# Attention with VectorE casts into rows with a gap, a scaled v that goes through PSUM, and another order of the tasks of attention

## The chip, the cores and the metric

One core of a Trainium2 chip runs the whole program. The engines are TensorE (PE; its weight loads are listed as PEld), VectorE (DVE), ScalarE (ACT), GpSimd (POOL) and SyncE (SP, which issues the DMAs). The metric is the device time of one execution in microseconds (us), taken as the median of three runs; lower is better.

## The reference

Three stages follow each other. First attention over 2 x 8 heads, 768 rows, width 64, with a mask: each row of q and k gets a bucket of 6 bits, and only equal buckets attend to each other.

```python
q_bits = (np.einsum('bhsd,dk->bhsk', q, proj) > 0)
k_bits = (np.einsum('bhsd,dk->bhsk', k, proj) > 0)
mask = q_bucket[:, :, :, None] == k_bucket[:, :, None, :]
scores = scale * np.matmul(q, k.transpose(0, 1, 3, 2))
scores = np.where(mask, scores, -1000000000.0)
scores = scores - np.max(scores, axis=-1, keepdims=True)
attn = np.exp(scores)
attn = attn / (np.sum(attn, axis=-1, keepdims=True) + 1e-09)
return np.matmul(attn, v)
```

Then two feed-forward layers on 1536 tokens (512 to 2048 to 512): in the first the middle is a rational function of h (degree 3 over degree 2), in the second it is h minus tanh(h).

## The kernel before

**Attention.** Work goes head by head (16 heads), and in a head in six tiles of 128 keys (j = 0 to 5). What a head needs:

- `split_hi` on ACT and `split_lo` on POOL make two parts, A and Bl, of the loaded k and q; `place` sends them by DMA to TA, TBk and TBq; `bits` (6 matmuls) and its output on DVE write the bucket bits into TBk, and a DMA copies 12 of these rows to TBq.
- `smax`: for each tile two matmuls (`sm`, line 456) and a DVE reduction over 768 columns (`mx`, line 460); when all six are done, `put_max` transposes the maxima (`mt`), DVE writes `mr`, and a DMA puts them into TBq.
- `scores`: for each tile four matmuls (`st`, line 582) into PSUM, then ACT's exponential into an f32 tile `e` (line 585).
- `round_e` rounds `e` to f16 (`eh`). `EH_ACT` says how many of the 768 columns ACT takes in each of the six tiles, 768, 768, 128, 768, 512, 768; DVE casts the rest (line 593), so 640 columns in tile 2 and 256 in tile 4. `rest_e` forms `el = e - eh` on POOL (line 602). The last head has tables of its own (`EH_ACT_LAST`, `EL_DVE_LAST`), by which DVE does some of the `el`.
- `attend`: 18 matmuls for each tile (`pv`, lines 634 to 637), with pieces of `eh` and `el` as weights.
- v is scaled by a power of two and split in two: `vhi` on ACT (line 548), `vlo` on DVE in one instruction that reads v and the high part, both in SBUF (line 557; heads 0 and 1 take ACT and POOL). `vmean_of` makes the mean over v.

**PSUM.** `double` gives one of three buffers of two banks, used in turn by `sm`, `st`, `bits`, `xT`, the shifted weight words (`low`) and, at the end, `hr`. So a matmul into the next buffer waits until the engine that reads the third last one is done. `single` gives one bank for small things; one more bank holds `pv`.

**What sets the order.** Every task gets a place on a common scale (one unit is one tile j, six are a head): the tables `T` and `EARLY` give its offset, lines 686 to 748 make the list, and lines 749 and 750 sort it and record the instructions in this order. Each engine runs its own instructions strictly in that order; semaphores are set from the data. `fill` (line 607) issues matmuls on constants into an unused part of the `pv` bank; `FILL` says where and how many.

**Seam.** While the last heads run, the weights of the first layer are prepared (ACT `scale`, DVE `low` and `wt`, lines 187 and 192, ACT and POOL halves). After the last scores four `hr` tiles (unit 0 of the first layer) and the rest of `pv` run, then the last `xT` transposes, then `h` of unit 1 begins. From there on a planner of the same kind (`NUDGE` shifts single tasks) orders the two layers.

Of the kernel before, what the change touches and what calls it, by code (L numbers as in the profile page):

```python
# [11 lines left out]
AF = mybir.ActivationFunctionType  # L12
# [21 lines left out]
M = dict(a=1, b=3.35, c=3.69, d=5, e=5, y=1.59, scale=3.71, join=3.82, halves=6.35)  # L34
# [16 lines left out]
EARLY = {0: dict(load=-61.69, hi=-62.14, lo=-60.39, place=-60.58, bits=-58.96, bits_out=-57.68, place_a=-58.4,
                lead=52.54, put=-46.37, v=-63.23, vmax=-58.62, vall=-56.52, vscale=-54.29, vhi=-6.88,
                vlo=-6.75, vmean=-5.12, vmean_out=-2.89, vback=-56.49, vagain=-55.68, put_half=-47.77,
                ls=0.86),
         1: dict(load=-67.13, hi=-65.44, lo=-65.19, place=-64.04, bits=-59.08, bits_out=-58.81, place_a=-57.52,
                lead=54.94, ls=1.12),
         2: dict(load=-64.89, hi=-61.91, lo=-61.61, place=-61.57, place_a=-61.53, bits=-58.68, bits_out=-58.14,
                lead=9.66, v=-20.61, ls=1.03),
         3: dict(load=-22.52, hi=-15.52, lo=-14.68, place=-14.44, place_a=-13.73, bits=-12.32, bits_out=-11.43,
                lead=9.64)}  # L60
NE = 1
T_LAST = dict(norm=9.87, x=10.11, x_out=10.68)

# [21 lines left out]
 'x_hi 0 5 0': -0.33,  # L85
 't_sum 1 5 0 3': -0.73}
GC = dict(sub=0.7, hi=1.35, lo=1.95)
# [35 lines left out]
def tile_fn(ctx: ExitStack, tc: tile.TileContext, kq, v, proj, w1i, w1o, a_, b_, w2i, w2o, out):  # L123
# [197 lines left out]
    with ExitStack() as actx:  # L321
# [228 lines left out]
        def vlo(h):  # L550
            t = VB[h % 3]
            if h in VLO_POOL:
# [65 lines left out]
        def attend(h, j):  # L618
# [561 lines left out]
```

## Time and profile before

| what | us |
|---|---|
| median of 3 runs (lowest, highest) | 766.49 (766.38, 767.56) |
| the profiled execution: time, span of its instructions | 770.33, 768.5 |
| PE busy, share of the span | 740.6, 96% |
| DVE busy | 625.3, 81% |
| POOL busy | 556.4, 72% |
| ACT busy | 492.6, 64% |

The profile is of one execution, a little slower than the median; its span leaves out 1.83 us around the instructions. Busy shares are means over stages with different limits; a matmul's end is modelled, so a busy PE can still contain short waits. The clock shown (PEclk) is the share of full speed that TensorE was granted.

### The profile page before, as it was taken

How to read it: one execution, taken by the hardware profiler on the slowest of the kernel's cores; microseconds unless marked ns; L12 is line 12 of the kernel's file. 1: busy time of each engine (PE TensorE's matmuls, PEld its weight loads, DVE VectorE, ACT ScalarE, POOL GpSimd, SP SyncE). 2: the span in 40 equal slices, each digit the busy share in tenths (PEclk: the TensorE clock that was granted, in tenths of full speed). 3: DMA queues.
4: the chain of work that ended last, by engine and by line, in shares of the span. 5: the costliest groups of instructions: out<-in, count | busy, mean ns of one | idle time of the engine just before them, and what ended most of it. 6: DMA issues, size and time to landing. Idle time of an engine off the chain costs nothing.

```text
span 768.5 us, 13965 instructions
## 1 busy us (share of the span) xinstructions
PE 740.6 (96%) x5273; PEld 639.6 (83%) x5273; DVE 625.3 (81%) x988; ACT 492.6 (64%) x831; POOL 556.4 (72%) x458
## 2 busy tenths in 40 slices
PE   5999999999998899999999999999999999999997
PEld 3888888888786788888888888887989899989886
DVE  6688999999988888879899998999656766767655
ACT  2577888878896788776666677767554354344421
POOL 3498999898998687787777789968555465465621
PEclk9699999999999999999999999999999999999999
DMA  7573546537421231121121212201031220311003
GB/s 195 147 181 108 146 130 166 158 93 191 119 85 55 71 95 56 55 82 56 57 81 56 82 29 64 73 1 56 27 110 41 70 82 28 110 55 55 28 28 137
DMA packets 41051, 66.52 MB, mean 87 GB/s; under 512 B 3844, under 2 KB 27492, under 8 KB 40984
## 3 DMA queue, kind: packets, MB, share of 16 engines
q1 hardware_dynamic: 40984, 65.63, 29.4%
q8 instruction: 41, 0.67, 0.4%
q14 instruction: 26, 0.21, 0.1%
HBM read 43.00 MB, written 3.15 MB: 60 GB/s over the span
## 4 chain that ended last, share of the span: by engine, by line
PE 77%; DVE 12%; POOL 4%; issue 2%; ACT 2%; DMA 1%; SPq 0%; ACTq 0%; DVEq 0%; POOLq 0%
PE y L1005 17%; PE y L784 12%; PE h L262 12%; PE st L582 7%; PE h2b L922 6%; PE h2e L922 4%; PE h2a L922 4%; PE sm L456 3%; DVE mx L460 3%; PE bits L431 2%; PE hr L262 2%; PE pv L634 1%; PE pv L635 1%; DVE eh L593 1%; PE pv L637 1%
## 5 line engine op out<-in xcount | busy, mean ns | idle before, releaser
L602 POOL TENSOR_TENSOR el<-e,eh 128x768 f16<-128x768 f32 (+1 forms) x95 | 158.8, 1687 | 26.1 <-ACT eh L591 15.1
L1005 PE MATMUL y<-wO,G 128*128 128x512 f32 x576 | 145.1, 393 | 0.3 <-POOL G L990 0.3
L990 POOL TENSOR_TENSOR G<-tmp,G 128x384 fp32r<-128x384 f32 x64 | 66.1, 1034 | 95.6 <-ACT G L985 85.6
L1005 PEld LDWEIGHTS y<-wO,G 128*128 128x128 f32 x576 | 107.0, 188 | 19.1 <-POOL G L990 0.8
L585 ACT ACTIVATE e<-st,lnk 128x768 f32<-128x768 f32 x96 | 86.2, 899 | 29.8 <-PE st L582 26.6
L460 DVE TENSOR_REDUCE mx<-sm 128x1 f32<-128x768 f32 x96 | 90.2, 951 | 9.6 <-PE sm L456 8.4
L1020 DVE TENSOR_TENSOR ya<-y,ya 128x512 f32<-128x512 f32 x84 | 58.1, 692 | 34.5 <-PE y L1005 34.5
L318 POOL TENSOR_TENSOR G<-vec,G 128x512 fp32r<-128x512 f32 x44 | 57.1, 1304 | 26.1 <-ACT G L313 26.0
L591 ACT CAST eh<-e 128x768 f16<-128x768 f32 (+2 forms) x93 | 65.8, 708 | 1.9
L784 PE MATMUL y<-G,wO 128*128 128x512 f32 x288 | 66.7, 389 | 0.0
L784 PE MATMUL y<-G,wE 128*128 128x512 f32 x288 | 66.3, 389 | 0.0
L262 PE MATMUL h<-x,wO 128*128 128x512 f32 x288 | 66.3, 389 | 0.0
L582 PE MATMUL st<-TA 128*128 128x384 f32 x192 | 57.5, 381 | 6.3 <-DVE wt L192 3.3
L784 PEld LDWEIGHTS y<-G,wE 128*128 128x128 f32 x288 | 54.1, 188 | 11.2
L262 PEld LDWEIGHTS h<-x,wO 128*128 128x128 f32 x288 | 54.1, 188 | 11.2
L784 PEld LDWEIGHTS y<-G,wO 128*128 128x128 f32 x288 | 54.0, 188 | 11.1
L634 PEld LDWEIGHTS <-eh 128*128 128x128 f16 x576 | 53.4, 97 | 9.2 <-issue 8.7
L634 PE MATMUL pv<-VB,eh 128*128 128x65 f16 x540 | 59.5, 195 | 0.0
L635 PE MATMUL pv<-VB,eh 128*128 128x64 f16 x540 | 59.1, 196 | 0.0
L637 PE MATMUL pv<-VB,el 128*128 128x65 f16 x540 | 58.6, 193 | 0.4 <-POOL el L602 0.4
L922 PE MATMUL h2b<-x,wE 128*128 128x384 f32 x288 | 58.1, 336 | 0.6 <-DVE tmp L938 0.6
L456 PE MATMUL sm<-TBk,TBq 76*128 76x384 f32 x192 | 54.7, 372 | 3.4 <-DVE mx L460 2.0
(170 smaller groups left out, 1877.4 us busy)
## 6 DMA issues: line engine op xcount, KB each, us to landing
raw<-in_w1i_dram SPq DMA_DIRECT2D x16, 512.0 KB
raw<-in_w1o_dram SPq DMA_DIRECT2D x16, 512.0 KB
raw<-in_w2i_dram SPq DMA_DIRECT2D x16, 512.0 KB
raw<-in_w2o_dram SPq DMA_DIRECT2D x16, 512.0 KB
kq<-in_kq_dram SPq DMA_DIRECT2D x16, 384.0 KB
TA<-A SPq DMA_DIRECT2D x32, 192.0 KB
TA<-Bl SPq DMA_DIRECT2D x32, 192.0 KB
vraw<-in_v_dram SPq DMA_DIRECT2D x8, 384.0 KB
```

What stands on the lines that cost most here:

```text
L262: nc.tensor.matmul(ps, l[:, dc], r, start=(n == 0), stop=(n == 11))
L456: nc.tensor.matmul(ps[:, n], TBq[h][0:76, j * P:(j + 1) * P], TBk[h][0:76, n * SH:(n + 1) * SH], start=True, stop=True)
L460: d = nc.vector.tensor_reduce(mx[h][:, j:j + 1], ps, axis=AX.XY, op=ALU.max)
L582: nc.tensor.matmul(ps[:, n], l[h][0:k, j * P:(j + 1) * P], q[h][0:k, n * SH:(n + 1) * SH], start=(k == P), stop=(k < P))
L585: outs["e", (h, j)] = lambda: nc.scalar.activation(halved(e), ps, AF.Exp, scale=1.0 / math.sqrt(D), bias=lnk)
L602: nc.gpsimd.tensor_sub(el[h, j][:, n:S], e[:, n:S], eh[h, j][:, n:S])
L634: nc.tensor.matmul(out(t), a[:, q], vb[:, j, 0:PW], start=False, stop=False, skip_group_check=True)
L635: nc.tensor.matmul(out(t)[:, 0:D], a[:, q], vb[:, j, PW:PW + D], start=False, stop=False, skip_group_check=True)
L637: nc.tensor.matmul(out(t), l[:, q], vb[:, j, 0:PW], start=False, stop=(j == NK - 1), skip_group_check=True)
L784: nc.tensor.matmul(ps, l[:, o], r, start=(n == 0), stop=(n == 11))
L922: nc.tensor.matmul(banks[n, k], w_in(j, l)[:, o:o + P], x[:, r, dt], start=new and z == 0, stop=z == 5, skip_group_check=not new)
L1005: nc.tensor.matmul(ps, g[:, l, o], r, start=(z == 0), stop=(z == 5))
```

## The change

It does six things.

1. `EH_ACT` gives ACT 384 columns of tile 4 (before 512), so DVE casts 384 (before 256); tile 2 stays at 640 on DVE. In tiles that DVE shares, `eh` is laid out in rows of 128 with a pitch of 130 (`EP`), so that DVE's casts write 5 and 3 rows of 128 with a gap of two elements, from one unbroken run of `e`.
2. `vlo` (heads 2 to 15): ACT writes the scaled v into columns 0 to 383 of the single bank, now one fixed tile `sbank`, and DVE subtracts the high part from it. `single` hands out columns 384 to 511 of the same bank.
3. In `vall` the maximum over a pair of heads is written to SBUF instead of PSUM.
4. The last head's tables: DVE gets `el` of 640, 640 and 512 columns and fewer casts.
5. `FILL`: nine places instead of three, 205 matmuls instead of 96.
6. New numbers in `T`, `EARLY`, `T_LAST` and ten more `NUDGE`s; a function `before` only asserts that the sorted tasks stand in a legal order.

```diff
-EH_ACT = (768, 768, 128, 768, 512, 768)
+EH_ACT = (768, 768, 128, 768, 384, 768)
+EP = P + 2
-EH_ACT_LAST = (0, 0, 768, 0, 640, 768)
-EL_DVE_LAST = (128, 0, 0, 128, 128, 768)
-FILL = ((1.54, 30), (100.1, 16), (200, 50))
+EH_ACT_LAST = (128, 0, 768, 768, 768, 768)
+EL_DVE_LAST = (640, 0, 0, 640, 512, 0)
+FILL = ((1.54, 28), (199.95, 68), (102.13, 12), (-62.29, 25), (-56.14, 20), (-45.0, 12), (92.46, 26), (-26.05, 8),
+ (55.32, 6))
...
+        sbank = sgl.tile([P, 512], F32, name="sbank")
+        user = []
         def single(name):
-            return sgl.tile([P, 512], F32, name=name, tag="s")
+            user[:] = [name]
+            return sbank[:, SH:512]
+        def still(name):
+            assert user == [name], (user, name)
...
             def back():
-                m = ps[0:2, P + 8:P + 9]
-                nc.vector.tensor_reduce(m, ps[0:2, 0:P], axis=AX.X, op=ALU.max)
-                nc.vector.tensor_mul(dg, ident[0:2, 0:2], m.to_broadcast([2, 2]))
+                still(f"vt{pr}")
+                nc.vector.tensor_reduce(dg[:, 2:3], ps[0:2], axis=AX.X, op=ALU.max)
+                nc.vector.tensor_mul(dg[:, 0:2], ident[0:2, 0:2], dg[:, 2:3].to_broadcast([2, 2]))
...
         def vlo(h):
...
-            nc.vector.scalar_tensor_tensor(out=t[:, :, D + 1:2 * D + 1], in0=vsl(h), scalar=vsc[h],
-                                           in1=t[:, :, 0:D], op0=ALU.mult, op1=ALU.subtract)
+            x = sbank[:, 0:SH].rearrange("p (t d) -> p t d", t=NK)
+            nc.scalar.activation(x, vsl(h), AF.Copy, scale=vsc[h])
+            nc.vector.tensor_sub(t[:, :, D + 1:2 * D + 1], x, t[:, :, 0:D])
...
         def round_e(h, j):
-            eh[h, j] = ap.tile([P, S], F16, name=f"eh{h}_{j}", tag="eh", bufs=6)
+            t = ap.tile([P, NK * EP], F16, name=f"eh{h}_{j}", tag="eh", bufs=6)
             n = (EH_ACT if h < BH - 1 else EH_ACT_LAST)[j]
+            w = P if n == S else EP
+            t = eh[h, j] = t[:, 0:NK * w].rearrange("p (t w) -> p t w", w=w)[:, :, 0:P]
+            r, e = n // P, ef[h, j].rearrange("p (t w) -> p t w", w=P)
             if n:
-                nc.scalar.copy(eh[h, j][:, 0:n], ef[h, j][:, 0:n])
+                nc.scalar.copy(t[:, 0:r], e[:, 0:r])
             if n < S:
-                nc.vector.tensor_copy(eh[h, j][:, n:S], ef[h, j][:, n:S])
+                nc.vector.tensor_copy(t[:, r:NK], e[:, r:NK])
```

Three places show how the order moves. The first is DVE in the opening, from the bits of head 1 to the bits of head 2 (`mx_211` and `mx_257` are the maxima of head 0, `mx_248` and `mx_316` those of head 1). Before:

```order
L441 TENSOR_SCALAR TBk_183<-bits_200,thr,amp 44x768
L460 TENSOR_REDUCE mx_211<-sm_4_245 128x1
L460 TENSOR_REDUCE mx_248<-sm_0_249 128x1
L460 TENSOR_REDUCE mx_211<-sm_5_254 128x1
L476 TENSOR_SCALAR mr_0_263<-mt_0_261 3x128
L460 TENSOR_REDUCE mx_248<-sm_1_258 128x1
L460 TENSOR_REDUCE mx_248<-sm_2_267 128x1
L476 TENSOR_SCALAR mr_3_280<-mt_3_278 3x128
L441 TENSOR_SCALAR TBk_237<-bits_270,thr,amp 44x768
```

And now:

```order
L537 TENSOR_SCALAR TBk_210<-bits_239,thr,amp 44x768
L556 TENSOR_REDUCE mx_257<-sm_4_291 128x1
L573 TENSOR_SCALAR mr_0_299<-sbank 3x128
L556 TENSOR_REDUCE mx_257<-sm_5_295 128x1
L573 TENSOR_SCALAR mr_3_311<-sbank 3x128
L537 TENSOR_SCALAR TBk_282<-bits_303,thr,amp 44x768
L556 TENSOR_REDUCE mx_316<-sm_0_317 128x1
```

The three maxima of head 1 that stood ahead of the last `mr` of head 0 now stand behind it.

The second is DVE in a middle head (tile 4 of head 4; `VB` is the low part of v). Before:

```order
L460 TENSOR_REDUCE mx_1125<-sm_2_1244 128x1
L593 CAST eh_4_1271<-e_4_1238 128x256
L570 SCALAR_TENSOR_TENSOR VM_147<-vm_1247,VM_147 32x64
L460 TENSOR_REDUCE mx_1125<-sm_3_1280 128x1
L441 TENSOR_SCALAR TBk_1234<-bits_1264,thr,amp 44x768
...
L557 SCALAR_TENSOR_TENSOR VB_138<-vraw_558,vsc_867,VB_138 128x6x64
```

And now:

```order
L556 TENSOR_REDUCE mx_1203<-sm_2_1310 128x1
L671 SCALAR_TENSOR_TENSOR VM_148<-sbank,VM_148 32x64
L537 TENSOR_SCALAR TBk_1314<-bits_1319,thr,amp 44x768
L697 CAST eh_4_1331<-e_4_1302 128x3x128
L658 TENSOR_TENSOR VB_139<-sbank,VB_139 128x6x64
L556 TENSOR_REDUCE mx_1203<-sm_3_1371 128x1
```

The bits of the next head stand ahead of the cast, and the low part of v directly behind it.

The third is ACT at the same place. Before:

```order
L585 ACTIVATE e_4_1238<-st_4_1239,lnk 128x768
L591 CAST eh_4_1271<-e_4_1238 128x512
L569 ACTIVATE VM_147<-vm_1247 64x64
L585 ACTIVATE e_5_1274<-st_5_1275,lnk 128x768
```

And now:

```order
L686 ACTIVATE e_4_1302<-st_4_1303,lnk 128x768
L670 ACTIVATE VM_148<-sbank 64x64
L695 CAST eh_4_1331<-e_4_1302 128x3x128
L657 ACTIVATE sbank<-vraw_619,vsc_946 128x384
L686 ACTIVATE e_5_1334<-st_5_1335,lnk 128x768
```

The copy of the scaled v is one instruction more between the exponentials of tiles 4 and 5.

On SP the copy of the bits to TBq now stands ahead of the four copies to TA of the same head, and no longer behind them. On PE the fills stand: 25 ahead of the first `bits`, 20 behind the first `vt` transpose, 12 and 8 among the maxima of head 1, 28 behind tile 1 of head 0, 6 in head 9, 26 behind tile 2 of the last head, and 80 in one row behind the last `xT` (before: 30 in head 0, 16 ahead of the last `xT` and 50 behind it).

## Rows read from the trace of the kernel before

**Rows 1.** Busy time by stretch: PE, PEld, DVE, ACT, POOL, then PEclk, DMA, GB/s.

```profile
225.35:260.16 34.81, 29.66 (x360) 25.14 (x356) 29.09 (x42) 25.74 (x42) 27.88 (x21) 0.95 0.14 47
260.16:768.50 508.34, 501.90 (x2352) 432.05 (x2352) 399.44 (x629) 295.74 (x539) 344.35 (x312) 1.00 0.20 64
```

**Rows 2.** The same view from head to head (first scores to first scores).

```profile
26.57:215.25 188.68, 182.39 (x2357) 161.50 (x2355) 169.16 (x265) 156.86 (x231) 167.47 (x99) 0.98 0.53 142
...
54.02:68.18 14.16, 14.16 (x172) 12.80 (x172) 11.88 (x20) 9.95 (x15) 10.86 (x8) 0.88 0.29 68
...
81.96:94.42 12.46, 12.46 (x174) 11.39 (x172) 11.80 (x22) 10.97 (x18) 11.20 (x8) 1.00 0.47 115
94.42:107.86 13.44, 13.32 (x177) 11.66 (x175) 12.16 (x18) 11.47 (x18) 12.79 (x8) 1.00 0.62 167
...
146.16:160.61 14.45, 13.70 (x178) 11.73 (x176) 13.73 (x18) 12.26 (x20) 12.95 (x8) 1.00 0.48 131
```

**Rows 3.** Timeline around 52 us: start, length, engine, line, tiles, wait before.

```profile
50.80 1.65 POOL L602 TENSOR_TENSOR el<-e,eh 128x768 f16<-128x768 f32 x1
50.99 1.60 DVE L593 CAST eh<-e 128x256 f16<-128x256 f32 x1
...
52.88 1.08 DVE L441 TENSOR_SCALAR TBk<-bits,thr,amp 44x768 fp32r<-44x768 f32 x1
...
54.02 0.62 PE L582 MATMUL st<-TA 128*128 128x384 f32 x2 [1.37 <-DVE TBk L441]
```

**Rows 4.** Busy time by stretch of 2 us, behind that stall.

```profile
56.00:58.00 2.00, 2.00 (x10) 1.74 (x10) 0.91 (x2) 1.53 (x2) 1.04 (x2) 0.50 0.67 193
```

**Rows 5.** Groups of DVE by form: count, busy us, mean ns, idle before.

```profile
L187 DVE TENSOR_SCALAR low<-raw 128x512 int32<-128x512 int32 x64 | 43.9, 686 | 0.1
...
L593 DVE CAST eh<-e 128x256 f16<-128x256 f32 x15 | 19.4, 1295 | 0.2 <-ACT e L585 0.2
...
L593 DVE CAST eh<-e 128x640 f16<-128x640 f32 x15 | 12.9, 862 | 1.0 <-ACT e L585 1.0
L557 DVE SCALAR_TENSOR_TENSOR VB<-vraw,vsc,VB 128x384 f16<-128x384 f32 x14 | 12.8, 916 | 0.2
...
L651 DVE TENSOR_TENSOR xt<-pv,rz 128x384 f32<-128x384 f32 x15 | 8.4, 557 | 0.5
```

**Rows 6.** DVE line 593 by itself: lengths in ns, least/median/most.

```profile
L593 DVE CAST eh<-e x34: 483/1017/1943, 34.9 to 238.8; 128x640 f16<-128x640 f32 x15, 128x256 f16<-128x256 f32 x15, 128x768 f16<-128x768 f32 x3, 128x128 f16<-128x128 f32 x1
```

**Rows 7.** DVE line 600 by itself, the same columns.

```profile
L600 DVE TENSOR_TENSOR el<-e,eh x4: 278/1094/1553, 230.6 to 240.4; 128x128 f16<-128x128 f32 x3, 128x768 f16<-128x768 f32 x1
```

**Rows 8.** ACT line 554 by itself, the same columns.

```profile
L554 ACT ACTIVATE vx<-vraw,vsc x2: 600/606/612, 17.1 to 31.6; 128x384 f32<-128x384 f32 x2
```

**Rows 9.** Timeline of PE in the opening.

```profile
26.57 0.99 PE L582 MATMUL st<-TA 128*128 128x384 f32 x2
...
29.28 3.08 PE L615 MATMUL pvw<-ones 128*128 128x122 f16 x30
...
32.22 0.60 PE L582 MATMUL st<-TA 128*128 128x384 f32 x2
```

**Rows 10.** Timeline of DVE in the opening.

```profile
14.76 6.14 DVE L460 TENSOR_REDUCE mx<-sm 128x1 f32<-128x768 f32 x7
...
23.57 0.28 DVE L476 TENSOR_SCALAR mr<-mt 3x128 fp32r<-3x128 f32 x1 [0.74 <-PE mt L471]
```

**Rows 11.** Timeline around the seam.

```profile
232.12 1.75 DVE L593 CAST eh<-e 128x768 f16<-128x768 f32 x1
...
235.35 0.59 PE L582 MATMUL st<-TA 128*128 128x384 f32 x2 [2.58 <-DVE wt L192]
```

**Rows 12.** Timeline of PE at the end of the seam.

```profile
255.81 2.83 PE L615 MATMUL pvw<-ones 128*128 128x122 f16 x50
260.16 2.12 PE L262 MATMUL h<-x,wE 128*128 128x512 f32 x8 [1.52 <-DVE g L308]
```

**Rows 13.** Timeline of PE at the entry of the second layer.

```profile
503.36 2.35 PE L922 MATMUL h2a<-x,wE 128*128 128x384 f32 x12 [1.43 <-ACT tmp L933]
```

More of the change, by code (lines that the diff above doesn't have):

```diff
@@ L51 @@
[L51 to L60, printed above, removed]
+T = {'load': -21.6,
+ 'hi': -16.1,
+ 'lo': -15.12,
+ 'place': -13.78,
+ 'place_a': -12.96,
+ 'bits': -13.59,
+ 'bits_out': -13.11,
+ 'put': -3.09,
+ 'put_out': -3.08,
+ 'vhi': -8.16,
+ 'vlo': -6.69,
+ 'vmean': -2.55,
+ 'vmean_out': -1.12,
+ 'lead': 9.84,
+ 'max': 0.3,
+ 'exp': 0.41,
+ 'round': 0.91,
+ 'rest': 1.08,
+ 'pv': (5.03, 6.95, 7.8, 8.64, 8.0, 9.16),
+ 'pv_last': (5.41, 6.77, 8.07, 9.01, 8.9, 9.11),
+ 'norm': 9.95,
+ 'x': 14.6,
+ 'x_out': 15.0,
+ 'v': -16.72,
+ 'vmax': -12.1,
+ 'vall': -10.56,
+ 'vscale': -9.62,
+ 'h0': 0.65,
+ 'slot': 0.93,
+ 'a': 0.78,
+ 'b': 2.0,
+ 'c': 2.29,
+ 'd': 4.03,
+ 'e': 4.29,
+ 'gates': 21.86,
+ 'vback': -10.2,
+ 'vagain': -9.93,
+ 'w_load': 7.03,
+ 'wt': (-41.69, -21.14, -17.84, -12.15, -6.33, -4.04, 0.32, 3.85),
+ 'ls': 0.98}
@@ new lines @@
+EARLY = {0: {'load': -61.72,
+     'hi': -61.83,
+     'lo': -60.39,
+     'place': -60.47,
+     'bits': -58.96,
+     'bits_out': -54.6,
+     'place_a': -58.76,
+     'lead': 52.4,
+     'put': -46.8,
+     'v': -63.23,
+     'vmax': -58.62,
+     'vall': -56.59,
+     'vscale': -54.29,
+     'vhi': -6.88,
+     'vlo': -6.21,
+     'vmean': -4.7,
+     'vmean_out': -2.89,
+     'vback': -56.5,
+     'vagain': -55.68,
+     'put_half': -47.77,
+     'ls': 0.87,
+     'x': 14.61},
+ 1: {'load': -66.87,
+     'hi': -65.63,
+     'lo': -65.13,
+     'place': -64.04,
+     'bits': -61.45,
+     'bits_out': -58.61,
+     'place_a': -57.52,
+     'lead': 51.27,
+     'ls': 1.45,
+     'vagain': -10.0,
+     'vlo': -3.71},
+ 2: {'load': -64.89,
+     'hi': -61.83,
+     'lo': -61.61,
+     'place': -61.6,
+     'place_a': -61.53,
+     'bits': -59.14,
+     'bits_out': -58.33,
+     'lead': 9.69,
+     'v': -20.69,
+     'ls': 1.13,
+     'vall': -10.56},
+ 3: {'load': -22.46,
+     'hi': -15.52,
+     'lo': -15.12,
+     'place': -14.51,
+     'place_a': -13.12,
+     'bits': -12.26,
+     'bits_out': -11.13,
+     'lead': 9.99,
+     'ls': 1.0}}
@@ L61 @@
 NE = 1
-T_LAST = dict(norm=9.87, x=10.11, x_out=10.68)
+T_LAST = {'norm': 9.87, 'x': 10.11, 'x_out': 11.11}
 NUDGE = {'stage_e 10 1': 1.68,
@@ L85 @@
  'x_hi 0 5 0': -0.33,
- 't_sum 1 5 0 3': -0.73}
+ 't_sum 1 5 0 3': -0.73,
+ 'x_hi 1 1 0': -0.21,
+ 'stage_c 11 1': 0.92,
+ 'stage_b 10 3': -0.56,
+ 'u2 0 0': -0.74,
+ 'join1 4 0': 0.76,
+ 'x_lo 0 5 0': -0.15,
+ 'y2_out 1 1': -0.02,
+ 'rest2 3 1': 2.41,
+ 'x_lo 0 0 0': 5.11,
+ 'scale2 3 1': -1.22}
 GC = dict(sub=0.7, hi=1.35, lo=1.95)
@@ L469, in put_part @@
         def put_part(h, m, t0, n):
-            ps = single(f"mt{h}_{t0}")[0:n, 0:P]
+            ps = single(f"mt{h}_{t0}")[0:n]
             nc.tensor.transpose(ps, m[:, t0:t0 + n], ident)
             def out():
+                still(f"mt{h}_{t0}")
                 mr = ap.tile([n, P], F32R, name=f"mr{h}_{t0}", tag="mr", bufs=2)
@@ L567, in out @@
             def out():
+                still(f"vm{h}")
                 t, c = VM[h % 3], 2.0 ** 14 * EPS / S
@@ L633, in attend @@
                 q = slice(t * P, (t + 1) * P)
-                nc.tensor.matmul(out(t), a[:, q], vb[:, j, 0:PW], start=False, stop=False, skip_group_check=True)
-                nc.tensor.matmul(out(t)[:, 0:D], a[:, q], vb[:, j, PW:PW + D], start=False, stop=False,
+                nc.tensor.matmul(out(t), a[:, t], vb[:, j, 0:PW], start=False, stop=False, skip_group_check=True)
+                nc.tensor.matmul(out(t)[:, 0:D], a[:, t], vb[:, j, PW:PW + D], start=False, stop=False,
                                  skip_group_check=True)
```

59 lines of the change are left out of this document (42 added, 17 removed).

## The prediction

> **What bounds the kernel now.** I read the busy times by stretch first, then those from head to head, then the timeline where a head is long, then the DVE groups by form. From 260.16 us on PE is busy for 501.90 of 508.34 us [rows 1]: the two layers are bound by matmuls, and the change hardly touches them. What can move is attention and seam, 0 to 260 us.
>
> In a middle head without disturbance PE is busy all the time, 12.46 of 12.46 us, and 13.32 of 13.44 us in the next, which also carries the transposes of a pair [rows 2]. So 12.95 us is what PE itself wants for a head, as the mean of the two. Fourteen heads took 188.68 us [rows 2] instead of 14 x 12.95 = 181.3: 7.4 us are lost to waits and to a low clock, in some heads only. The head at 146.16 us took 14.45 us, and DVE was busy for 13.73 of them [rows 2]. There DVE is the late engine, since the weights of the first layer pass through it as well.
>
> How DVE makes PE late stands in one place as an example [rows 3]. POOL works on `el` from 50.80 to 52.45; DVE's cast of 256 columns starts at 50.99 and ends 0.14 us after POOL, at 52.59. Behind it in the queue stands TBk, which empties a PSUM buffer; the next scores wait for it and start at 54.02, after 1.37 us without a matmul. [...]
>
> That the cast is held and not slow is seen from the groups: 256 columns took 1295 ns on average, 640 columns only 862 [rows 5], and the shortest cast 483 ns [rows 6]. The old `vlo` (two inputs in SBUF) took 916 ns, while an instruction of the same 384 columns with one input in PSUM took 557 [rows 5].
>
> **The change part by part.** *Casts.* Tile 4: 384 columns in 3 rows. No cast of this form stands in the trace. Bounds: below, that it runs as the shortest one, under 0.48 us; above, that it is still held as before, 1.3 us for the mean and 1.94 for the worst [rows 5, 6]. I take the pace of DVE operations at one column a cycle: 512 columns in 686 ns and 384 in 557 [rows 5], so 0.55 us for 384 and, by the same slope of 1.0 ns a column, 0.82 for 640. Tile 2 then gains 0.04 us in the mean and tile 4 0.75, and neither depends on POOL any more.
>
> [...]
>
> *vlo.* 916 ns become 557 by the row of the same size with one input in PSUM [rows 5]: 0.36 us of DVE. ACT pays: one copy of 384 columns, 0.61 us [rows 8], less about 0.1 for the 128 columns it gives up. Here the destination is PSUM and not SBUF, which I cannot price apart; I take the same. ACT was busy for 156.86 us in 14 heads, 11.2 of 13.5 us a head [rows 2], so 0.5 more is hidden at 11.7 of 12.95. It adds a wait too: DVE's subtraction waits for ACT's copy, and behind it on DVE stands the maximum of tile 3, for which the next `sm` waits. I count it at nothing, because DVE gets back 0.04 + 0.75 + 0.36 = 1.15 us a head. That cover is gone where the weights are prepared; then up to 0.6 us a head shows.
>
> *Order in the middle heads.* TBk now stands ahead of the cast of tile 4 (second fence of the change), so the stall of rows 3 should not occur even if the cast is slow. SP sends the bits ahead of the four copies to TA; those are needed by scores a head later, so their later issue is hidden. Of the 7.4 us of loss I take 60%, 4.5 us (range 1 to 6.5): the rest is short waits that another queue order makes anew.
>
> *Opening.* The last `mr` of head 0 stood behind nine maxima and now stands behind six. Seven took 6.14 us, 0.88 each [rows 10], so it ends 2.6 us earlier than 23.85. But the scores also stand behind all `sm` of head 1, which DVE paces, so I take 1.2 us off the first scores' start at 26.57 [rows 9]. From there 32.22 - 26.57 = 5.65 us go into eight score matmuls and 30 fills, which ran at 0.103 us each, against 2.83 / 50 = 0.057 later [rows 9, 12]. With the new fills ahead of them (25 + 20 + 12 + 8, all where PE waits for DMA or DVE) part of this may run at the full clock: up to 2.8 us, of which I take 0.8, since DVE's pace still leaves gaps. Together 2.0 (range 0 to 4.5).
>
> *Seam.* At 232 us a cast of 768 columns took 1.75 us, and the scores waited 2.58 us for the weight word behind it [rows 11]. Now DVE has ahead of that word a cast in 5 rows (0.82), an `el` of 640 (0.82) and a cast of 768 in 6 rows, an even count, which I leave at 1.75 as before. The `el` has two inputs in SBUF: line 600, 128 columns wide, took between 278 and 1553 ns [rows 7], so it too can be held, by 1.27 us. I take 2.0 us off the wait, less 0.5 that the 26 new fills (26 x 0.057 = 1.5) and the held `el` cost: 1.5 (range -1 to 3).
>
> [...]
>
> At the end of the seam nothing is won: 50 fills end at 258.64 and `h` waits until 260.16 [rows 12]; the 80 fills now behind `xT` last 80 x 0.057 = 4.6 us against 1.5 + 2.83, and `h` now waits for a weight word behind the same `g`.
>
> *Second layer.* `h2a` waits 1.43 us for ACT behind a chain of DVE [rows 13], and one subtraction of DVE (`x_lo 0 0 0`) is moved out of it, 5 us later, by its `NUDGE`: 0.5 us (range -0.5 to 1.4). *Fills* in the middle: 6 x 0.057 = 0.3 us more on a busy PE.
>
> **Sum.** 4.5 + 2.0 + 1.5 + 0.5 - 0.3 = 8.2 us. The profiled execution took 770.33 us, so it would take 762.1; the median of the runs is 3.84 lower, 766.49, and gives 758.3.
>
> **Rivals.**
> (a) *The relief is taken up by the next wait.* ACT and POOL are close behind: POOL was busy for 167.47 us in 14 heads, 12.0 us of the 12.95 that PE wants [rows 2]. If they set the pace in half of the heads, two thirds of the 4.5 are lost: 8.2 - 3.0 = 5.2 less at best; with the opening unchanged (2.0), 3.2: 763.3 us. Against it: el itself does not grow, and POOL too waits less when casts end early.
> [...]
> (c) *Slower: ACT's copy falls on the path.* It stands between the exponentials of tiles 4 and 5, and each exponential frees a PSUM buffer for coming matmuls. If PE waits for it in each of 14 heads, it costs 14 x 0.6 = 8.4 us, and each stall can bring a stretch at the lower clock as in rows 4; with three of these, 1.0 us each (2 us at half the clock), it is 11.4 against 8.2: 766.49 + 3.2 = 769.7. It decides once ACT needs more than the 12.95 us of PE, that is 1.2 us more than my 11.7, in most heads; so far it needs that at most in the stretch from 146 us on, where it was busy for 12.26 of 14.45 [rows 2].
> (d) *More than forecast*: the opening at full clock (4.5), all of the middle (6.5), the seam 3: 15 with the rest, 751.5.
>
> **How the numbers follow.** Forecast 0.60, (a) 0.13, (b) 0.08, (c) 0.10, (d) 0.06, nothing that can be told 0.03. About 0.2%, 1.5 us, is what a measurement of this kernel tells from no change. Faster by more: forecast, (a), (b), (d), less 0.02 from their edges: 0.85. Within: 0.05. Slower: 0.10. The likeliest case by itself reaches from 754 to 762. The range goes to 752 for (d), and to 766 to take in (a) and (b) with the upper bounds of their terms; (c) is left out.
>
> **What would show it.** Right: in the profile after, casts of 384 near 0.55 us and of 640 near 0.82 with hardly any spread; `VB` on DVE near 0.56; the head at 146 us near 13.4; no stretch at half clock near 56 us; first scores near 25 us. Wrong: casts that still spread from 0.5 to 1.9 us (b); ACT above 12.5 us a head and PE waiting for `e` (c); first scores at 26.5 with the clock at half until 32. I would be wrong as a whole if the heads, although DVE waits less, still take 13.4 us and more.

## Result and the profile after

The changed kernel takes 757.52 us (median of 4 runs, 756.77 to 761.38) against 766.62 us for the kernel before in the same session: a ratio of 0.9889, 95% interval 0.9859 to 0.9918. Its profiled execution is the slowest of the four, 761.38 us with a span of 759.6. A second session gave 757.00 us (754.63 to 757.55) and a ratio of 0.9852 (0.9834 to 0.9871). That profile (754.63 us, span 752.9) is of the fastest of its four executions, so the two bracket the others. Stages are compared below within profiled executions, from the first scores of one head to those of another. So that they can be added, this is the first one against that of before:

| stretch | before, us | after, us | difference | predicted |
|---|---|---|---|---|
| start to first scores | 26.57 | 25.88 | -0.7 | -1.2 |
| heads 0 and 1 | 27.45 | 30.46 | +3.0 | -0.8 (clock) |
| heads 2 to 14 | 171.33 | 163.51 | -7.8 | -4.5, fills +0.3 |
| head 15 to first `h` (seam) | 34.81 | 31.43 | -3.4 | -1.5 |
| `h` to the end | 508.34 | 508.32 | 0.0 | -0.5 |
| sum | 768.5 | 759.6 | -8.9 | -8.2 |

Busy time by stretch of the kernel after; columns as in [rows 1]. The stretches are heads 0 and 1, head 2, head 3, the head that answers to 146.16 of [rows 2], fourteen heads, the seam, and all that follows:

```profile
25.88:56.34 30.46, 28.40 (x282) 25.82 (x278) 18.71 (x32) 22.42 (x34) 20.67 (x13) 0.78 0.40 117
56.34:69.15 12.81, 12.57 (x179) 11.46 (x175) 11.92 (x22) 10.98 (x17) 11.44 (x7) 1.00 0.49 129
69.15:81.62 12.47, 12.47 (x176) 11.74 (x176) 10.43 (x18) 11.71 (x19) 11.43 (x7) 1.00 0.62 164
145.05:158.00 12.95, 12.95 (x183) 11.90 (x182) 11.54 (x20) 12.39 (x20) 12.32 (x8) 1.00 0.60 157
25.88:209.18 183.30, 179.13 (x2363) 163.89 (x2360) 155.68 (x265) 160.49 (x244) 159.83 (x99) 0.96 0.54 146
219.85:251.28 31.43, 29.80 (x400) 25.89 (x397) 24.34 (x41) 26.82 (x45) 25.58 (x21) 1.00 0.16 52
251.28:759.60 508.32, 501.83 (x2355) 432.21 (x2352) 396.62 (x629) 295.69 (x539) 344.29 (x312) 1.00 0.20 64
```

A head with the transposes of a pair takes 12.47 us now (69.15 us), where [rows 2] had 13.44 (94.42 us). Head 2, without them, took 14.16 behind the stall of [rows 3] and takes 12.81. Over fourteen heads DVE is busy 155.68 us instead of 169.16, ACT 160.49 instead of 156.86. The stretch that lost is the first: heads 0 and 1 at a mean clock of 0.78.

DVE by form in the kernel after (count, busy us, mean ns, idle before), against [rows 5]:

```profile
L697 DVE CAST eh<-e 128x640 f16<-128x640 f32 x16 | 13.0, 812 | 2.8 <-ACT e L686 2.8
L697 DVE CAST eh<-e 128x384 f16<-128x384 f32 x15 | 8.3, 554 | 0.5
L658 DVE TENSOR_TENSOR VB<-sbank,VB 128x384 f16<-128x384 f32 x14 | 7.8, 560 | 0.5
L610 DVE TENSOR_TENSOR vdg<-ident,vdg 2x2 f32<-2x2 f32 x8 | 6.2, 781 | 0.3
L704 DVE TENSOR_TENSOR el<-e,eh 128x640 f16<-128x640 f32 x2 | 1.8, 886 | 0.1
```

The casts and `VB` have the durations that the prediction gave (0.82, 0.55, 0.56). The fourth row is a cost that it did not count: `vdg` is the product of `ident` and the maximum of v (`back` in the diff), which now takes that maximum from SBUF, and this product of 2x2 elements takes 0.78 us in the mean, up to 1.65, where it took 0.145 before.

The opening of this execution, in PE's timeline and by stretch:

```profile
27.02 0.51 PE L683 MATMUL st<-TBq,TBk 77*128 77x384 f32 x2
29.59 0.27 PE L605 MATMUL sbank<-ident,vm 128*2 128x128 f32 x1 [2.06 <-DVE vm L596]
29.70 2.30 PE L719 MATMUL pvw<-ones 128*128 128x122 f16 x28
```

```profile
26.00:30.00 4.00, 1.94 (x17) 1.64 (x16) 2.42 (x5) 3.79 (x6) 1.29 (x1) 1.00 0.82 282
32.00:44.00 12.00, 12.00 (x67) 10.70 (x68) 6.44 (x12) 7.62 (x12) 8.13 (x7) 0.50 0.40 99
54.00:58.00 4.00, 4.00 (x57) 3.67 (x57) 3.87 (x7) 3.48 (x7) 3.56 (x3) 1.00 0.42 105
```

PE waits 2.06 us for the maximum of the second pair's v, and from 32 to 44 us it works without a break at a granted clock of 0.50, where the kernel before had 1.00 from 32 us on. The stall of [rows 3] and the half clock of [rows 4] at 54 to 58 us are gone.

### The profile page after: what moved, and what is told of

The parts are those of the page before. It is cut to its first block, busy times and chain, and to the rows that moved or that the text cites. A ratio compares the mean times of both kernels' runs of the same rounds, so it can differ in the third digit from the quotient of the medians.

```text
span 759.6 us, 14193 instructions
## 1 busy us (share of the span) xinstructions
PE 740.5 (97%) x5382; PEld 645.3 (85%) x5382; DVE 604.4 (80%) x985; ACT 497.9 (66%) x847; POOL 546.2 (72%) x459
## 4 chain that ended last, share of the span: by engine, by line
PE 71%; DVE 15%; POOL 4%; ACT 4%; DMA 2%; issue 2%; SPq 0%; ACTq 0%; POOLq 0%; DVEq 0%
PE y L1140 17%; PE y L919 14%; PE h L351 13%; PE h2b L1057 7%; DVE mx L556 5%; PE h2e L1057 4%; PE h2a L1057 4%; PE st L683 3%; PE sm L552 2%; ACT e L686 2%; PE bits L527 1%; DVE TBk L537 1%; POOL G L407 1%; POOL wE L976 1%; DVE eh L697 1%
## 5 line engine op out<-in xcount | busy, mean ns | idle before, releaser
L706 POOL TENSOR_TENSOR el<-e,eh 128x768 f16<-128x768 f32 (+2 forms) x96 | 152.8, 1610 | 29.3 <-ACT eh L695 13.0
L556 DVE TENSOR_REDUCE mx<-sm 128x1 f32<-128x768 f32 x96 | 89.4, 949 | 15.5 <-PE sm L552 14.8
L919 PEld LDWEIGHTS y<-G,wO 128*128 128x128 f32 x288 | 54.0, 188 | 11.1
L738 PE MATMUL pv<-VB,eh 128*128 128x65 f16 x540 | 57.8, 193 | 0.0
L739 PE MATMUL pv<-VB,eh 128*128 128x64 f16 x540 | 57.4, 195 | 0.0
```

The lines of the kernel that those rows point to most:

```text
L556: d = nc.vector.tensor_reduce(mx[h][:, j:j + 1], ps, axis=AX.XY, op=ALU.max)
L706: nc.gpsimd.tensor_sub(l[:, r:NK], e[:, r:NK], eh[h, j][:, r:NK])
L738: nc.tensor.matmul(out(t), a[:, t], vb[:, j, 0:PW], start=False, stop=False, skip_group_check=True)
L919: nc.tensor.matmul(ps, l[:, o], r, start=(n == 0), stop=(n == 11))
```

## Experiments

All ratios are to the kernel before in the same session. "Middle" is heads 2 to 14, from the first scores of head 2 to those of head 15 in the profiled execution.

| kernel | casts | vlo | order | median, us | ratio (95%) | middle, us |
|---|---|---|---|---|---|---|
| before | one run | old | old | 766.5 to 768.2 | 1 | 171.3 |
| after, again | gap | PSUM | new | 757.00 | 0.9852 (0.9834 to 0.9871) | 163.5 |
| nogap | one run | PSUM | new | 764.32 | 0.9956 (0.9940 to 0.9971) | 171.1 |
| evenrows | gap, 6 and 2 rows | PSUM | new | 766.67 | 0.9983 (0.9972 to 0.9993) | 172.2 |
| gap_t2 | gap in tile 2 only | PSUM | new | 757.96 | 0.9865 (0.9842 to 0.9887) | 162.5 |
| vlo_old | gap | old | new | 759.88 | 0.9893 (0.9867 to 0.9918) | 164.7 |
| order_alone | one run | old | new | 770.70 | 1.0037 (1.0022 to 1.0052) | 171.3 |
| before_gap | gap | old | old | 768.26 | 0.9996 (0.9977 to 1.0014) | 166.4 |
| gap_bank | gap, not in head 12 | old | old | 764.85 | 0.9959 (0.9944 to 0.9974) | 167.0 |
| old_order | gap | PSUM | old | 773.85 | 1.0068 (1.0043 to 1.0094) | 172.5 |
| old_order_vlo | gap | PSUM, earlier | old | 772.88 | 1.0058 (1.0037 to 1.0080) | 175.0 |
| fill_first | gap | PSUM | new | 757.76 | 0.9857 (0.9835 to 0.9880) | 164.1 |
| fill_vdg | gap | PSUM | new | 755.08 | 0.9824 (0.9802 to 0.9845) | 161.7 |

### after_again: the changed kernel a second time

> The changed kernel once more, to see whether the opening of its first profile is the rule. In that profile PE stood for 2.06 us ahead of 29.59 us, until v of the second pair had come and DVE had its maximum, and then TensorE had 0.50 of its clock from about 31 to 44 us, with PE busy all the time; that execution took 761.4 us, the others 756.8 to 758.0. Theory: the low stretch is there in every execution and only its length differs, so a profile of some 757 us shows it shorter (clock 0.50 for 6 to 10 us instead of 13). Rival: it is an accident of that one execution; then the clock stays at 1.00 from 24 us on. Time by both: 757.5 us, 756.5 to 761.

By stretch:

```profile
14.00:21.00 7.00, 6.22 (x25) 4.11 (x24) 5.28 (x8) 1.85 (x3) 2.67 (x2) 0.57 0.94 226
30.00:44.00 14.00, 13.37 (x161) 11.64 (x161) 10.18 (x16) 13.04 (x20) 13.10 (x9) 1.00 0.51 141
25.33:49.64 24.31, 22.68 (x281) 20.31 (x278) 19.56 (x32) 22.47 (x34) 20.56 (x13) 1.00 0.49 138
49.64:213.13 163.49, 160.56 (x2244) 146.63 (x2240) 143.84 (x246) 148.13 (x226) 148.93 (x93) 1.00 0.54 145
```

The rival was right on the stretch: 1.00 from 30 to 44 us. Heads 0 and 1 took 24.31 us instead of 30.46, and all of the 6.7 us between the two spans lies before head 2; the middle agrees within 0.02 us. So the opening is decided by the execution (head 2 starts at 49.6 to 56.3 us), the middle is not. PE's wait for the maximum of v was shorter here, 0.99 us instead of 2.06, and the clock did not fall behind it:

```profile
27.98 0.27 PE L605 MATMUL sbank<-ident,vm 128*2 128x128 f32 x1 [0.99 <-DVE vm L596]
```

### nogap and evenrows: what the gap and the odd count do

```
-EP = P + 2
+EP = P
```

> The changed kernel with the gap taken out (rows of eh 128 wide again, so source and destination of every cast are one run). Theory: the casts are held by POOL again; 384 columns spread from about 0.4 to 1.9 us with a mean above 0.9, 640 columns from 0.48 to 1.9; DVE is busier by some 10 us in 16 heads, POOL's el spreads up to 2.0 us as before, and the time rises by 2 to 5 us, to about 761. Rival: the new order made the gain and hides the held casts: the spread returns and the time stays within 1.5 us of 757.5.

```
-EH_ACT = (768, 768, 128, 768, 384, 768)
+EH_ACT = (768, 768, 0, 768, 512, 768)
```

> The gap stays, but DVE casts 768 columns of tile 2 (6 rows) and 256 of tile 4 (2 rows) in place of 640 (5 rows) and 384 (3 rows): the same columns, even counts of rows. [...] Rival: any gap between rows is enough: 768 columns take 0.95 us and 256 take 0.43 with hardly any spread, time 757 to 758.

DVE's casts by form, in nogap and then in evenrows, and what PE waited for in nogap (us in total, times, longest):

```profile
L697 DVE CAST eh<-e 128x640 f16<-128x640 f32 x16 | 22.0, 1374 | 2.9 <-ACT e L686 2.8
L697 DVE CAST eh<-e 128x384 f16<-128x384 f32 x15 | 6.9, 461 | 0.5
```

```profile
L697 DVE CAST eh<-e 128x768 f16<-128x768 f32 x16 | 23.3, 1455 | 2.1 <-ACT e L686 2.1
L697 DVE CAST eh<-e 128x256 f16<-128x256 f32 x15 | 7.6, 506 | 0.5
```

```profile
PE sbank L664 <- DVE mr L573: 5.9, 8, 1.3
```

Without the gap the 640 columns are held (1.37 us in the mean, against 0.81 in after), and `mr` behind them in DVE's queue lets PE wait 5.9 us. The middle loses nearly all that it had won, 7.6 of 7.8 us, for 9.0 us more in the casts of tile 2. The gap with even counts does the same: 768 columns at 1.46 us and not the 0.95 of the rival. The shortest casts tell the same: 256 columns in 2 rows took 0.294 us at the least and 384 in one run 0.359, against 0.55 in 3 rows. Lengths of DVE line 697 (least/median/most), in evenrows and then in nogap:

```profile
L697 DVE CAST eh<-e x32: 294/833/2036, 34.1 to 230.0; 128x768 f16<-128x768 f32 x16, 128x256 f16<-128x256 f32 x15, 128x640 f16<-128x640 f32 x1
L697 DVE CAST eh<-e x32: 359/836/1948, 32.4 to 226.2; 128x640 f16<-128x640 f32 x16, 128x384 f16<-128x384 f32 x15, 128x768 f16<-128x768 f32 x1
```

So in these casts it is the odd count that helps, not the gap as such: in after the 5 rows took 0.81 to 0.82 us and the 3 rows 0.55 to 0.56, every one of them. Why the count decides is not shown. Against the expectation, tile 4 was hardly held: 384 columns took 0.46 us in the mean, less than with the gap. In the profile of after only 4 of its 15 casts overlap with work of POOL, while all 16 casts of 640 columns do.

### gap_t2: the gap in tile 2 alone

```
-            w = P if n == S else EP
+            w = EP if j == 2 else P
```

> The changed kernel with the gap in tile 2 alone (640 columns in 5 rows); the 384 columns of tile 4 are cast in one run. The prediction put the gain of the casts on tile 4 (0.75 us a head) and next to nothing on tile 2 (0.04). Theory now: in the new order it is tile 2 that POOL would hold; without a gap tile 4 takes 0.46 us in the mean, so it gains 0.1 us and loses nothing: the middle 162.5 to 164.5 us, the time 756 to 758. Rival (the prediction's own account): tile 4 is held again, above 0.9 us in the mean, the middle grows by 2 to 5 us and the time is 759 to 762.

```profile
L697 DVE CAST eh<-e 128x640 f16<-128x640 f32 x16 | 14.1, 881 | 2.6 <-ACT e L686 2.4
L697 DVE CAST eh<-e 128x384 f16<-128x384 f32 x15 | 6.9, 460 | 0.5
```

The theory holds: the middle is 162.45 us, 1.1 less than in after, and the time that of the changed kernel. The edit also takes the gap from the casts of the last head; there the one of 640 columns took 1.91 us, and the seam is 32.73 us instead of 31.43, which takes that gain back. The prediction had the gain on the wrong tile. In the old order tile 4 stood against POOL's `el` (1.30 us for 256 columns, [rows 5]); in the new order tile 2 stands against work of POOL (1.37 us for 640 columns in nogap).

### order_alone and old_order: each half of the change

The first is the changed kernel with casts in one run, tile 4 split 512 to 256, and the old `vlo`:

```
-EH_ACT = (768, 768, 128, 768, 384, 768)
-EP = P + 2
+EH_ACT = (768, 768, 128, 768, 512, 768)
+EP = P
...
-            nc.vector.tensor_sub(t[:, :, D + 1:2 * D + 1], x, t[:, :, 0:D])
+            nc.vector.scalar_tensor_tensor(out=t[:, :, D + 1:2 * D + 1], in0=vsl(h), ...)
```

The second has both edits and all tables of before (EH_ACT_LAST, T, EARLY, T_LAST and NUDGE as well):

```
-EL_DVE_LAST = (640, 0, 0, 640, 512, 0)
+EL_DVE_LAST = (128, 0, 0, 128, 128, 768)
-FILL = ((1.54, 28), (199.95, 68), (102.13, 12), ...
+FILL = ((1.54, 30), (100.1, 16), (200, 50))
...
```

> The new tables alone: the new places, fills and splits, with casts in one run and tile 4 split 512 to 256 as before, and the old vlo. Theory (order gives only opening and seam): the middle 171 to 173 us, the time 763 to 766, as without the gap or up to 1.5 us more for the old vlo. Rival (the order carries the gain that was predicted for the middle): under 168 us in the middle and 760 or less in all.

> Both edits (casts in odd rows with a gap, scaled v through PSUM) with all tables of the kernel before: places, early places, fills, NUDGE and the split of the last head. From the first scores of head 2 to those of head 15 the kernel before took 171.3 us, the changed one 163.5, and the changed one without the gap 171.1. Theory: the edits alone carry the middle, whatever the order, since no cast is held any more: 164 to 166 us there, and the time 759 to 762 (opening and seam stay as before the change). Rival: the edits gain only together with the new order, which puts the casts and the weights' tasks where DVE has room: over 168 us in the middle and 764 to 767 in all.

Each half alone is slower than before, and only together do they gain. Neither is a bare half: both keep the one shared bank and the maximum in SBUF (items 2 and 3 of the change), and in order_alone PE waits 2.6 us for `vdg`. In order_alone the middle is what the theory said, 171.3; the 770.7 was not foreseen. In old_order the middle is the rival's, and the time lies beyond both. What waits in old_order (PE, then DVE):

```profile
PE sbank L527 <- DVE VB L570: 5.6, 6, 1.3
PE h L263 <- DVE g L309: 5.0, 1, 5.0
PE sbank L527 <- DVE vdg L522: 4.0, 2, 3.4
```

```profile
DVE VB L570 <- ACT sbank L569: 9.8, 12, 1.4
```

The prediction counted DVE's wait for ACT's copy at nothing. In the new order it is: the row of `VB` above shows 0.5 us of idle time in all 14. In the old order it is 9.8 us, with the maxima behind it, and PE waits 5.6 us more for the bank that is shared now. That is rival (c) in another form: not ACT's load, but DVE's wait for it.

### old_order_vlo: is it the place of `vlo`?

```
-vhi=-8.38, vlo=-3.99
+vhi=-8.16, vlo=-6.69
```

> Both edits in the old order, as in old_order, with two places moved to those of the changed kernel: vlo from -3.99 to -6.69 and vhi from -8.38 to -8.16. In old_order DVE waited 9.8 us in all for ACT's copies to PSUM, with the maxima behind it that the next sm need, and PE 5.6 us for the bank that VB's subtraction still held. Theory: the place of vlo is what made the edits useless in the old order: the middle falls from 172.5 to 164 to 166.5 us, DVE's wait for the copy below 2 us, and (since hr(0,3) lies in another bank than h(1,0) here) the time to 761 to 764. Rival: the middle is spoiled by the order as a whole: over 169.5 us, and the time 766 or more.

```profile
PE sbank L527 <- DVE vdg L522: 8.3, 5, 2.8
PE st L595 <- ACT e L598: 3.3, 7, 0.8
```

```profile
DVE VB L570 <- ACT sbank L569: 9.1, 14, 0.7
```

```profile
L522 DVE TENSOR_TENSOR vdg<-ident,vdg 2x2 f32<-2x2 f32 x8 | 7.3, 913 | 0.3
```

These are PE's waits, DVE's, and the group of `vdg`. The theory fell. DVE still waited 9.1 us for the copies, the waits for the shared bank moved to `vdg` (0.91 us in the mean, PE waits 8.3 us behind it), and the middle grew to 175.0. That the tables as a whole make the edits pay in the middle is shown (172.5 against 163.5 us with the same edits); which of its other places do it is open.

### before_gap and gap_bank: the gap alone, and what ate its gain

before_gap is the kernel before with the changed kernel's casts:

```
-EH_ACT = (768, 768, 128, 768, 512, 768)
+EH_ACT = (768, 768, 128, 768, 384, 768)
+EP = P + 2
...
-                nc.vector.tensor_copy(eh[h, j][:, n:S], ef[h, j][:, n:S])
+                nc.vector.tensor_copy(t[:, r:NK], e[:, r:NK])
```

gap_bank leaves head 12 in one run:

```
-            w = P if n == S else EP
+            w = EP if h != 12 and n < S else P
```

> The kernel before with one edit alone: casts in 5 and 3 rows with a gap (and tile 4 split 384 to 384). vlo is still one DVE operation with two inputs in SBUF. Theory: 640 columns at 0.81 us and 384 at 0.55 without spread; the middle takes 165 to 167 us in place of 171.3 (vlo, 0.92 us on average, still costs some), the time 761 to 763. Rival (order needed, or vlo the main load): the casts are short, and yet the middle stays over 169 and the time within 1.5 us of 767.6.

> The kernel before with the gap in its casts, as in before_gap, but head 12 keeps casts in one run. This leaves the order of every engine as it was and changes one thing more: which of three PSUM buffers the four hr get. In before_gap, h(1,0) lies in a bank that hr(0,3) leaves last, so PE waited 4.99 us for the fourth g of DVE where the kernel before waited 1.52 for the third, and ran on at half clock (seam 2.4 and what follows 2.8 us longer); here that bank is left by hr(0,2), as in the kernel before. Theory: the middle keeps the gain of the gap (166 to 167.5 us against 171.3), the wait of h is about 1.5 us again, what follows takes 508.4, and the time is 762 to 764.5. Rival: the seam is late for another reason (an earlier attention only waits longer for the weights); then h still starts near 258 and the time stays at 767 to 769.

In before_gap the casts are short (0.81 and 0.55 us) and the middle falls by 4.9 us, which is the theory; the time does not move. Heads 0 and 1 give back 0.65 us: in head 1 the old `vlo` took 5.89 us (4.90 in gap_bank) while POOL worked without a break, and that head took 16.3 us (15.5) instead of 14.2. From the timelines of DVE and POOL:

```profile
42.35 5.89 DVE L558 SCALAR_TENSOR_TENSOR VB<-vraw,vsc,VB 128x384 f16<-128x384 f32 x1
38.02 8.03 POOL L606 TENSOR_TENSOR el<-e,eh 128x768 f16<-128x768 f32 x5
45.99 1.84 POOL L407 TENSOR_TENSOR Bl<-kq,A 128x768 fp32r<-128x768 f32 x1
```

The larger loss comes later. Its end of the seam, against [rows 12], and what follows:

```profile
250.44 2.83 PE L619 MATMUL pvw<-ones 128*128 128x122 f16 x50
258.26 13.97 PE L263 MATMUL h<-x,wE 128*128 128x512 f32 x48 [4.99 <-DVE g L309]
```

```profile
260.00:264.00 4.00, 4.00 (x11) 3.04 (x11) 0.83 (x2) 0.97 (x3) 1.82 (x2) 0.50 0.80 239
258.26:769.40 511.14, 504.68 (x2352) 434.05 (x2352) 396.17 (x624) 294.94 (x537) 342.44 (x310) 0.99 0.20 62
```

PE, DVE, ACT and POOL run their instructions in the same order as before. But another `hr` lies in the bank that `h` needs: `h` waits 4.99 us for the fourth `g` (DVE's last reading of an `hr`) instead of 1.52 for the third, and runs at half clock from 260 to 264 us. In gap_bank, with the bank as before:

```profile
220.88:253.49 32.61, 28.05 (x360) 23.88 (x356) 26.98 (x42) 25.75 (x42) 27.15 (x21) 1.00 0.15 50
253.49:761.80 508.31, 501.90 (x2352) 432.05 (x2352) 399.47 (x629) 295.76 (x539) 344.32 (x312) 1.00 0.20 64
```

Seam 32.61 instead of 37.24 us, the rest 508.31 instead of 511.14, and the median 764.85, 0.35 us above the range of the theory, whose account holds. The medians, of two sessions, differ by 3.4 us, the two profiled executions by 7.5 in these stretches (that of before_gap is the slowest of its ten). order_alone and old_order have the same bank: in their profiles `h` waits 2.9 and 5.0 us, and what follows it is 1.3 and 1.5 us longer than 508.4. So some of their slowness is this accident and not the half of the change that they test. Their middles, 171.3 and 172.5, are free of it.

### vlo_old: what `vlo` through PSUM is worth

Here DVE's one operation on v and `VB` comes back, with two inputs in SBUF:

```
-            nc.scalar.activation(x, vsl(h), AF.Copy, scale=vsc[h])
-            nc.vector.tensor_sub(t[:, :, D + 1:2 * D + 1], x, t[:, :, 0:D])
+            nc.vector.scalar_tensor_tensor(out=t[:, :, D + 1:2 * D + 1], in0=vsl(h), scalar=vsc[h],
+                                           in1=t[:, :, 0:D], op0=ALU.mult, op1=ALU.subtract)
```

> The changed kernel with the old vlo: one DVE operation on v and VB, both in SBUF, without ACT's copy to PSUM. Theory: it is held by POOL, 0.6 to 1.95 us, 0.9 in the mean and so 0.35 us more per head on DVE; where DVE is late PE waits for it, the middle takes 164.5 to 167 us instead of 163.5 and the time is 758 to 760.5. Rival: DVE has room in every head now, ACT is relieved by 0.58 us a head: the middle stays at 163.5 and the time within 1 us of 757.

The middle is 164.70 us, 1.2 above that of after, and the time 759.88: the theory, at the low end of its price, since the operation took 0.64 us in the new order and not 0.92 (the row below). Another 1.4 us lie in the seam (32.80 instead of 31.43 us), where the last head's cast of 768 columns took 1.63 us and not 0.76.

```profile
L656 DVE SCALAR_TENSOR_TENSOR VB<-vraw,vsc,VB 128x384 f16<-128x384 f32 x14 | 9.0, 644 | 0.0
```

### fill_first and fill_vdg: the opening

```
-FILL = ((1.54, 28), ...
+FILL = ((1.4, 28), ...
```

> The 28 fills that stand behind the transpose of v's maxima (vt of the second pair) stand ahead of it, in the stretch where PE waited 2.06 us. Theory: the idle time there brought the clock to 0.50 from 31 to 44 us; with the fills in it PE stands for under 0.6 us, the clock stays at 1.00, and the 28 fills no longer delay the scores behind them. Head 1 starts 3 to 5 us earlier than 44.56, and the time falls by 2 to 4 us, to about 754.5. Rival: DVE and the arrival of v set the pace of the first two heads, as before the change; then head 2 starts where it did (56.3) and the time stays within 1 us of 757.5.

The time did not move, as the rival said; but the execution profiled had lost its clock earlier, at 0.50 from 18 to 30 us:

```profile
18.00:30.00 12.00, 11.75 (x63) 9.60 (x62) 8.12 (x11) 2.31 (x4) 1.44 (x2) 0.50 0.80 201
```

So it does not tell whether the fills at 29 us would have held it. What came ahead of that loss were short waits of PE between the first `sm` (0.24 to 1.05 us each in after). fill_vdg fills them, and keeps the maximum in PSUM:

```
- (55.32, 6))
+ (55.32, 6), (-51.5, 12), (-50.63, 5), (-49.76, 5), (-48.89, 5), (-47.2, 8))
-                nc.vector.tensor_reduce(dg[:, 2:3], ps[0:2], ...)
+                nc.vector.tensor_reduce(sbank[0:2, 0:1], ps[0:2], ...)
```

> A version that may beat the changed kernel: 35 more fills between the first sm, from 11 to 17 us, where PE stood 0.24 to 1.05 us at a time; and the maximum of v's scale is kept in PSUM again (in the free part of the bank that vlo uses), so that the product with ident has one input in SBUF, not two. Theory: TensorE's clock fell at 14.5 to 16.6 us after those idle stretches and came back at 20 to 30, later in some executions than in others; with PE busy it stays at 1.00 until 26, head 2 starts at 49.6 or earlier in every execution and the runs lie closer together; vdg takes 0.15 us each time in place of 0.15 to 1.65, and PE's wait of 1.4 us for it goes, so the middle takes 162.5 to 163.3: the time is 753.5 to 755.5. Rival: the fills stand in the way of sm, or DVE paces the opening anyway: head 2 at 50 to 53 us, and the time 756.5 to 758.

```profile
10.00:18.00 8.00, 7.91 (x61) 6.65 (x61) 7.06 (x12) 1.86 (x3) 2.45 (x3) 1.00 0.80 189
18.00:28.00 10.00, 7.40 (x57) 4.78 (x55) 7.97 (x12) 2.34 (x4) 0.71 (x1) 1.00 0.91 230
28.00:32.00 4.00, 3.02 (x30) 2.99 (x30) 1.26 (x3) 2.27 (x4) 3.79 (x3) 0.60 0.29 112
52.16:213.89 161.73, 160.20 (x2243) 146.66 (x2240) 140.37 (x246) 148.13 (x226) 148.90 (x93) 1.00 0.54 146
```

```profile
L610 DVE TENSOR_TENSOR vdg<-ident,sbank 2x2 f32<-2x2 f32 x8 | 1.2, 144 | 0.3
```

It is the fastest of all: 755.08 us, with runs from 753.8 to 755.5, where the changed kernel's go from 754.6 to 761.4. Its interval and that of after_again overlap by a little (0.9834 to 0.9845), so about 2 us are likely rather than proven. The clock stays at 1.00 to 28 us as expected, then falls at a wait of 1.96 us at the same place as in after, and head 2 starts at 52.16, not at 49.6. `vdg` takes 0.144 us again and the middle 161.73, better than expected. Two things were changed at once here; the new fills all lie ahead of head 2, so the gain in the middle is put down to `vdg`.

## Why the prediction came out, step by step

*Casts.* Durations right: the pace of 1.0 ns a column, an estimate from two rows of [rows 5], gave 0.82 and 0.55 us, and 0.81 and 0.55 were measured. That casts in 5 and 3 rows do not depend on POOL no row of before showed; the profile after does, for its 16 casts of 640 columns took 0.81 to 0.82 us, all of them beside work of POOL. So the spread from 0.5 to 1.9 us that would have spoken for rival (b) is refuted. Casts that are held again cost most of the gain: nogap is 3.3 us faster than the kernel before in its session, though there tile 2 is held and not tile 4. The account by tile was wrong (0.75 us on tile 4, 0.04 on tile 2): it took which cast is held from the old order, and the change moved that.

*vlo.* DVE's price was right (0.56 us). Worth 1.2 us in the middle. The wait for ACT cost nothing only because of the new places; the cover that I named, DVE's 1.15 us, is there in old_order too, and the wait is not hidden there.

*Middle heads.* Mis-sized: -4.5 predicted, -7.8 measured from head 2 on, beyond its range of 1 to 6.5. The failed step is the base. I took 13.32 busy us of 13.44 in a head as PE's own work, so 12.95 as the mean. After, a head with those transposes takes 12.47, and in fill_vdg PE is busy 160.20 us for the same 13 heads, 12.3 each, where before it was 166.49:

```profile
54.02:225.35 171.33, 166.49 (x2231) 147.38 (x2232) 156.49 (x247) 143.97 (x212) 154.69 (x93) 0.99 0.50 134
```

Of these 6.3 us some 1.7 are the lower clock of [rows 4] (an estimate: 0.99 in the mean over 171.33 us). The other 4.6 looked like work and went with the waits, so they were, as far as this tells, short waits inside busy time. The loss to be won in these 13 heads was 171.33 - 160.20 = 11.1 us; the 7.4 was that of heads 0 to 13, two of which belong to the opening. The share was low too: 7.8 of 11.1 is 70%, not 60%. Rival (d), with 6.5, was nearer.

*Opening.* -2.0 predicted. The first scores came near the forecast (25.4; measured 25.88 and 25.33). Head 2 started at 56.34 and 49.64 us in two executions of the same kernel, against 54.02: +2.3 and -4.4. The bounds (0 to 4.5 gained) miss the bad case: I did not see that PE now waits for v ahead of its 28 fills and can lose its clock there (0.50 from 32 to 44 us in the first execution). Whether another place of the fills would mend that is open, as fill_first could not tell. The rows of before come from an execution with a mean granted clock of 0.987, at 0.50 from 18.4 to 32 us; 18 of the 19 in the second session had 0.993 to 0.998, which leaves no room for 13.6 us at half clock in some 766. So the slow opening that the prediction read is not the usual one. The changed kernel had 0.990 or less in six of its eight executions, and fill_vdg 0.993 to 1.000 in its five.

*Seam.* -1.5 predicted, -3.4 measured, just past its range. Up to 1.7 us of it is clock (an estimate: 0.95 over 34.81 us before [rows 1], 1.00 after), which the prediction did not count here. The cast of 768 took 0.76 us where the prediction left 1.75 (that an even count of rows is held no row of before showed; evenrows shows it for tile 2, 1.46 us in the mean), and the new `el` of 640 and 512 columns 0.69 to 0.94. That is partly luck, as it hangs on what they meet: the cast took 1.63 us in nogap and in vlo_old, and the `el` of 512 columns 1.41 in nogap. The 1.27 us by which the prediction let an `el` be held are the spread of [rows 7]; in the changed kernel no such hold shows on the `el`, but one of up to 1.5 us does on `vdg` (0.15 to 1.65 us, and 0.144 with one input in PSUM).

*POOL as the next limit (rival a).* Not seen: its busy time fell too, from 167.47 us in fourteen heads to 159.83, and no wait of PE in heads 2 to 14 of after ends with POOL.

*Second layer.* -0.5 predicted, nothing measured: `h2a` (the first matmuls of that layer) waits 1.46 us for ACT, as in [rows 13]; moving `x_lo 0 0 0` did not touch that wait.

*Sum.* The `vdg` term was missing; fill_vdg's middle is 1.8 us shorter without it. The sum came within 0.7 us of the difference between the two profiles since the middle and the seam won 5.5 us more than forecast (the fills counted in), and the opening and the second layer 4.8 less. So the direction was right, and the closeness of the number is luck.

## What to carry to other kernels

Test each half of a joint change before crediting either: here the edits alone cost 0.7%, the order alone 0.4% (an unlucky bank, the shared bank and the maximum in SBUF included in both), and both together gain 1.1 to 1.5%, because the order decides which operation meets which. When an edit that clearly works moves no time, look at what the allocation moved: a cast's new shape gave one PSUM bank another predecessor and cost 3.4 us at the far end. A row of busy PE is no floor; compare it with the shortest head, here 12.46 us before the change, which heads with the transposes reach too (12.47) once the waits are gone.

## What the runs showed that was not expected

A product of 2x2 elements on DVE with both inputs in SBUF took 0.15 to 1.65 us beside work of POOL (eight in the changed kernel); with one input in PSUM the eight of the kernel before took 0.144 to 0.146, and those of fill_vdg 0.144 in the mean. A long one ends with the POOL operation that it met, here both at 61.60 us (the changed kernel):

```profile
60.86 0.74 DVE L610 TENSOR_TENSOR vdg<-ident,vdg 2x2 f32<-2x2 f32 x1
58.32 3.28 POOL L706 TENSOR_TENSOR el<-e,eh 128x768 f16<-128x768 f32 x2
```

Nor is a hold limited to one operation of POOL: the `vlo` of 5.89 us in before_gap lasted through four that followed each other.

One program starts head 2 at 49.6 us in one execution and at 56.3 in another, as the clock falls to 0.50 from 15 us on in the first and from 17 and from 30.5 us on in the second, each time after waits of PE (0.24 to 1.05 us between the first `sm`, and 2.06 us ahead of 29.59); in fill_vdg, where PE was busy for 7.91 of the 8 us from 10 to 18, it was 1.00 to 28 us.
